# From the fifth expert round on, token rows are turned by VectorE after a trip through DRAM instead of by TensorE

## The chip, the core and the metric

One Trainium2 chip, one core of it. The engines are TensorE (PE; its weight loads are listed apart as PEld), VectorE (DVE), ScalarE (ACT), GpSimd (POOL) and SyncE (SP), which issues most DMAs. Each engine works through its own instructions in program order. The metric is the device time of one execution in microseconds (us).

## What is computed

Attention over 8 sequences of 576 tokens with 8 heads gives 4608 rows of 512 numbers. Each row goes to exactly one of 8 experts, by taking the highest gate logits of all (token, expert) pairs first until an expert has its 576 tokens:

```python
x = attn_out.transpose(0, 2, 1, 3).reshape(B * S, H * D)      # 4608 x 512
logits = x @ w_gate
order = np.argsort(-logits.flatten())
for idx in order:
    tok, e = idx // E, idx % E
    if assigned[tok] >= 0 or counts[e] >= cap: continue       # cap = 576
    assigned[tok] = e; counts[e] += 1
for e in range(E):
    mask = assigned == e
    out[mask] = np.maximum(x[mask] @ w1[e], 0.0) @ w2[e]      # 512 -> 1024 -> 512
```

## The kernel before

**Attention** fills about the first 200 us. It leaves the rows in DRAM (`xd`) and the gate logits in SBUF. **The expert stage** follows, in eight rounds `r` = 0 to 7, each of one expert: which expert fills up next, and with which tokens, is known only from the rounds before it.

A round has two products on TensorE. GEMM1 (`first`, L1387) makes `ph` from the turned rows `xh`, `xl` and the weights `w1h`, `w1l`: 8 blocks `f` of hidden units by two halves `j` of the tokens (256 and 320), 12 matmuls each. GEMM2 (L1432, L1435, L1437) makes `py` from `hb` and `w2h`, `w2l`: five tiles `m` of tokens (four of 128, one of 64) by 8 blocks `f`, 112 matmuls. Values are split into a high part (rounded by ScalarE) and a low part (the difference, by VectorE), so each product has three matmuls: ScalarE makes `w1h`, `w2h`, `xh`, the high half of `hb`; VectorE makes `w1l`, `w2l`, `xl`, the low half of `hb`.

Beside the products of a round run four chains of small work:

- **The search** for a later expert (`search`, `step`): two passes of four steps. In each, TensorE counts by 9 matmuls (`pz<-G,ohr`, L820) how many tokens lie above 16 thresholds, and VectorE (`step`, L857 to L870) turns the counts (`Q`), picks a threshold (`delta`), and makes the flags `G` for the next count. `above_base` then adds the threshold to `base` and lays out the next ones (`kb`) on VectorE. `copies` makes `ohr`, four copies of a mask.
- **The list** of an expert's tokens (`settle`, `listing`): VectorE works out flags `ge`, TensorE ranks them (`pz<-ge`, L1078, L1079), VectorE makes `oa` and six `ob`, TensorE places them (`ptx<-rx,ob`), VectorE reads `idx`.
- **The rows** (`gather`): GpSimd gathers five tiles of rows `xg` from `xd` by `idx` (L1336), TensorE turns each by four transposes into PSUM (`ptx<-const,xg`, L1350), ScalarE takes `xh` and VectorE `xl` from there. A round's rows are gathered and turned during GEMM2 of the round before it.
- **The weights**: SP loads them in 256 KB pieces `raw` (L1230).

The order of all this is set while the kernel is built: `Schedule` takes every operation with its cost, its dependences and a boost, runs them through a model of the engines, and writes each engine's instructions in the order found. On the chip the order is then fixed.

## Time and profile before

| | before |
|---|---|
| three runs | 672.52, 675.93, 676.17 us; median 675.93 us |
| the profiled execution's own time | 669.58 us |
| its span | 667.4 us |
| TensorE, VectorE, ScalarE, GpSimd busy in it | 94 %, 70 %, 43 %, 31 % |
| GEMM1 of rounds 3 and 4 | 386.1 to 413.7 us, 443.6 to 471.2 us |
| GEMM2 of rounds 3 and 4 | 413.7 to 443.6 us, 471.2 to 501.1 us |
| GEMM2 of rounds 5, 6 and 7 | 528.7 to 556.7 us, 583.1 to 611.1 us, 636.7 to 662.3 us |

The table's windows begin and end where TensorE passes from one product to the other. Busy time of TensorE is modelled at the ends of matmuls, so how long something takes there is best read from the start of one instruction to the start of the next.

### The profile page before, as it was taken

The page shows a single profiled execution, that of the slowest core. Times are in us where ns is not written, and L with a number is a line of the kernel's source. Part 1 is how long each engine was busy: PE and PEld are TensorE (multiplying, and loading weights), DVE is VectorE, ACT ScalarE, POOL GpSimd, SP SyncE. Part 2 cuts the span into 40 slices and gives each one's busy share as a digit, 9 for nine tenths or more (in the row PEclk, how much of TensorE's full clock was granted, in tenths as well). Part 3 has the DMA queues.
Part 4 walks back from the last instruction along what each step waited for, and adds up shares of the span by engine and source line. Part 5 has one row for each costly group of instructions (what it writes and reads, how often), then busy time and mean ns, then how long its engine had stood idle before and what let it go on. Part 6 is the DMA issues. An engine that isn't in the chain of part 4 may idle for free.

```text
span 667.4 us, 19062 instructions
## 1 busy us (share of the span) xinstructions
PE 630.1 (94%) x7517; PEld 550.4 (82%) x7519; DVE 468.6 (70%) x1582; ACT 287.5 (43%) x638; POOL 209.5 (31%) x316
## 2 busy tenths in 40 slices
PE   7898799999749999999999999999999999999996
PEld 6777788878636988998898799789879989988985
DVE  6668678888678784789899589779968935724210
ACT  4655465555304824754444236235423525424311
POOL 5447456664004317424104103210410321311011
PEclk9999999999857999999999999999999999999999
DMA  8988988884206937978146026214511764203001
GB/s 241 243 238 232 236 248 257 245 238 132 74 7 205 209 89 192 252 161 279 49 117 215 33 72 211 98 56 154 170 49 56 249 198 154 70 35 104 1 25 47
DMA packets 51673, 99.09 MB, mean 148 GB/s; under 512 B 7168, under 2 KB 17152, under 8 KB 51584
## 3 DMA queue, kind: packets, MB, share of 16 engines
q1 hardware_dynamic: 42240, 72.71, 37.0%
q0 software_dynamic: 9344, 25.17, 13.9%
q8 instruction: 59, 0.97, 0.6%
q14 instruction: 30, 0.25, 0.1%
HBM read 72.69 MB, written 18.87 MB: 137 GB/s over the span
## 4 chain that ended last, share of the span: by engine, by line
PE 70%; issue 13%; DVE 9%; DMA 5%; POOL 1%; ACT 1%; SPq 1%; POOLq 0%; DVEq 0%; ACTq 0%
PE ph L1387 27%; PE py L1432 20%; PE px L528 4%; PE pS L516 3%; PE px L587 2%; PE pz L820 2%; PE ptx L1350 2%; PE py L1435 2%; PE py L1437 2%; DVE xs L538 1%; POOL out L1458 1%; DMA xd<-xs 1%; PE pz L899 1%; DVE mx L451 1%; DVE L L621 1%
## 5 line engine op out<-in xcount | busy, mean ns | idle before, releaser
L1432 PE MATMUL py<-w2h,hb 128*128 128x512 f32 x512 | 170.9, 399 | 0.0
L1387 PE MATMUL ph<-xh,w1h 128*128 128x256 f32 (+1 forms) x512 | 139.6, 303 | 0.0
L1387 PE MATMUL ph<-xh,w1l 128*128 128x256 f32 (+1 forms) x512 | 136.3, 297 | 0.0
L1387 PE MATMUL ph<-xl,w1h 128*128 128x256 f32 (+1 forms) x512 | 136.0, 296 | 0.0
L1432 PEld LDWEIGHTS py<-w2h,hb 128*128 128x128 f32 x512 | 96.2, 188 | 19.2
L1212 ACT ACTIVATE hb<-ph 128x256 fp32r<-128x256 f32 (+2 forms) x192 | 59.7, 346 | 99.9 <-PE ph L1387 99.0
L1432 PE MATMUL py<-w2l,hb 128*128 128x512 f32 x256 | 100.0, 391 | 0.0
L1458 POOL DMA_INDIRECT out<-y,idx x40 | 41.5, 1037 | 186.1 <-ACT y L1212 132.7
L1387 PEld LDWEIGHTS ph<-xh,w1l 128*128 128x128 f32 x512 | 91.8, 190 | 0.0
L1387 PEld LDWEIGHTS ph<-xh,w1h 128*128 128x128 f32 x512 | 91.6, 190 | 0.3
L1387 PEld LDWEIGHTS ph<-xl,w1h 128*128 128x128 f32 x512 | 91.7, 190 | 0.0
L1408 DVE SCALAR_TENSOR_TENSOR hb<-ph,hb 128x320 fp32r<-128x320 f32 (+1 forms) x128 | 57.0, 452 | 27.7 <-ACT hb L1212 27.1
L470 ACT ACTIVATE E<-pS 128x384 f32<-128x384 f32 x96 | 46.1, 491 | 54.1 <-PE pS L516 52.4
L1212 ACT ACTIVATE y<-py 128x512 f32<-128x512 f32 (+1 forms) x40 | 23.9, 597 | 101.0 <-PE py L1432 84.8
L1432 PEld LDWEIGHTS py<-w2l,hb 128*128 128x128 f32 x256 | 48.3, 189 | 8.5
L516 PE MATMUL pS<-q,k 128*64 128x64 f32 x1152 | 54.0, 233 | 0.7 <-issue 0.7
L1336 POOL DMA_INDIRECT xg<-xd,idx x40 | 42.7, 1067 | 34.9 <-issue 27.3
L528 PE MATMUL px<-v,E 128*64 128x65 f32 x1152 | 49.0, 228 | 2.5 <-issue 1.8
L1213 DVE TENSOR_TENSOR xl<-ptx,xh 128x512 fp32r<-128x512 f32 (+1 forms) x36 | 22.9, 635 | 38.8 <-ACT xh L1212 38.8
L303 POOL COPY v<-v 32x520 f32<-32x520 f32 (+2 forms) x56 | 33.3, 619 | 52.1 <-DMA v<-in_vp 16.3
L528 PEld LDWEIGHTS px<-v,E 128*64 128x64 f32 x1152 | 43.5, 141 | 6.6 <-issue 4.0
L516 PEld LDWEIGHTS pS<-q,k 128*64 128x64 f32 x1152 | 46.0, 144 | 0.8 <-issue 0.8
(209 smaller groups left out, 1124.1 us busy)
## 6 DMA issues: line engine op xcount, KB each, us to landing
raw<-in_moe_w SPq DMA_DIRECT2D x128, 256.0 KB, 4.2
qs<-in_qp SPq DMA_DIRECT2D x16, 288.0 KB, 4.7
k<-in_kp SPq DMA_DIRECT2D x16, 288.0 KB, 3.4
...
w2l<-raw POOLq DMA_DIRECT2D x16, 256.0 KB, 4.8
...
```

The costliest lines, as they stand in the source:

```text
L303: f(t[:32, c0 + 1:c1 + 1], t[96:, c0:c1])
L470: e = self.op("ACT", 475, lambda j=j, pS=pS: nc.scalar.activation(self.E[:, 3 * j:3 * j + 3].rearrange("p c x -> p (c x)"), pS.tile[:, :38 ...
L516: x = nc.tensor.matmul(pS[64 * h:64 * h + 64, k, :, h], self.K[:, 32 * g:32 * g + 64], self.Q[:, g], start=False, stop=True, skip_group_ch ...
L528: x = nc.tensor.matmul(px[64 * h:64 * h + 64, c - c0, a], self.E[:, k, 64 * a:64 * a + 64], self.V[:, k, 2 * self.ui + a], start=True, sto ...
L587: x = nc.tensor.transpose(pt.tile[:, 128 * (c - c0):128 * (c - c0) + 128], xs[:, c, 2 * ui:2 * ui + 2].rearrange("p a d -> p (a d)"), C["i ...
L1212: act = lambda o, i, f=AF.Copy: nc.scalar.activation(o, i, f)
L1213: sub = lambda e, o, a, b: e.tensor_tensor(o, a, b, op=OP.subtract)
L1336: nc.gpsimd.indirect_dma_start(out=xg[:n], out_offset=None, in_=xd, in_offset=bass.IndirectOffsetOnAxis(ap=box[0][:n, m:m + 1], axis=0))
L1387: nc.tensor.matmul(o, a[:, d * 128:d * 128 + 128], b[:, d, c0:c1], start=((d, i) == pairs[0]), stop=((d, i) == pairs[-1]))
L1408: hl = op("DVE", 335 if j == 0 else 400, lambda: nc.vector.scalar_tensor_tensor(hb[:, CAP + c0:CAP + c1], o, 0.0, hb[:, c0:c1], op0=OP.max ...
L1432: nc.tensor.matmul(py, x, w, start=(f + i == 0), stop=(f == NF - 1 and i == 2))
L1458: s = nc.gpsimd.indirect_dma_start(out=out, out_offset=bass.IndirectOffsetOnAxis(ap=box[0][:n, m:m + 1], axis=0), in_=y[:n], in_offset=None)
```

## The change

For rounds `r` of at least `QUARTERS` = 4, `gather` hands each tile to the new function `spread`. The rows are gathered into one of two tiles (used in turn by the five), SP stores them in a DRAM scratch `rows`, SP loads them back by four DMAs into 32 partitions each in pieces of 512 bytes, so that one VectorE instruction, which transposes blocks of 32 x 32 (`STREAM_TRANSPOSE`), leaves the wanted layout in place. `xh` and `xl` are then made from SBUF. The features end up in another order over partitions, so `W1` of these rounds is read from a second array `in_moe_w1q`, of equal size and with equal loads.

`above_base` is issued after `step`, and from the search for round `KB` = 4 on it goes to ScalarE; the cost of a step on VectorE in the planner falls with it. `copies` goes to ScalarE in all rounds but the first. The loads of `W1` of round 1 get a latency in the planner. `POOLED` is an empty range, so its branch is never taken.

```diff
-    def above_base(self, it, last, delta):
-        if it > 0:
+    def above_base(self, it, last, scalar):
+        nc, pw, delta = self.tc.nc, self.pw, self.delta
+        if it == 0:
+            self.base = delta
+        else:
             nb = pw.tile([128, 1], F32, name="base")
-            nc.vector.tensor_tensor(nb, self.base, delta, op=OP.add)
+            if scalar:
+                nc.scalar.activation(nb, delta, AF.Identity, bias=self.base)
+            else:
+                nc.vector.tensor_tensor(nb, self.base, delta, op=OP.add)
             self.base = nb
         if it < 2:
             kt = self.kstep(it + 2, last)
-            nc.vector.tensor_scalar(self.kb, kt, self.base, None, op0=OP.add)
+            if scalar:
+                nc.scalar.activation(self.kb, kt, AF.Identity, bias=self.base)
+            else:
+                nc.vector.tensor_scalar(self.kb, kt, self.base, None, op0=OP.add)
...
-                g = [chain("DVE", T_S + (725 if it == 3 and not v else -805 if it == 3 else 0), dve, [p], early)]
+                cost = T_S + (725 if it == 3 and not v else -805 if it == 3 else 0) - (250, 400, 150, 0)[it] * (r >= KB)
+                g = [chain("DVE", cost, dve, [p, *g[1:]], early)]
+                if it < 3 and r >= KB:
+                    g.append(chain("ACT", (190, 370, 190)[it], lambda v=v, it=it: R.above_base(it, v, True), g, early))
...
-                src = w1[bass.ds(E[r], 1), f].rearrange("o p d f -> p (o d f)")
+                src = (w1 if r < QUARTERS else w1q)[bass.ds(E[r], 1), f].rearrange("o p d f -> p (o d f)")
...
-        ld = op("SP", 60, load, [*deps, *old], dma=T_W)
+        ld = op("SP", 60, load, [*deps, *old], dma=T_W, lat=T_L if n == "1" and r == 1 and r in gate else 0)
...
-            oc = chain("DVE", 440, lambda: R.copies(R.oh), [lv])
+            oc = (chain("ACT", 1055, lambda: R.copies(R.oh, nc.scalar), [lv]) if r else
+                  chain("DVE", 640, lambda: R.copies(R.oh, nc.vector), [lv]))
...
+    def spread(r, m, n, a, b, wx, full, ix, box):
+        rows, k = XG[NM + m % 2], n // 32
+        xg = XG[m][:, :128 * k]
+        def get():
+            nc.gpsimd.indirect_dma_start(out=rows[:n], out_offset=None, in_=xd,
+                                         in_offset=bass.IndirectOffsetOnAxis(ap=box[0][:n, m:m + 1], axis=0))
+        g = op("POOL", 1250, get, [ix, *XU[NM + m % 2]], B_G, lat=T_B)
+        back = ROWS[r % 2][m]
+        sd = op("SP", 400, lambda: nc.sync.dma_start(back[:n], rows[:n]), [g, *RU.get((r - 2, m), [])], B_R, dma=T_W)
+        def move():
+            for q in range(4):
+                nc.sync.dma_start(xg[32 * q:32 * q + 32].rearrange("t (x c) -> t x c", x=k),
+                                  back[:n, 128 * q:128 * q + 128].rearrange("(x t) c -> t x c", t=32))
+        ld = op("SP", 1600, move, [sd, *XU[m]], B_R, dma=T_W)
+        RU[r, m] = [ld]
+        XU[NM + m % 2] = [sd]
+        t = op("DVE", 130 + 7 * n, lambda: nc.vector.transpose(xg, xg), [ld], B_T)
...
+        s0 = op("ACT", full, lambda: act(a, xt), [t, *wx], B_T)
+        s1 = op("DVE", full + 100, lambda: sub(nc.vector, b, xt, a), [s0], B_T)
```

What the planner made of it stands in the order of the instructions. On **VectorE**, in GEMM2 of round 3, the rows of round 4 and the search for round 5 meet. The first five rows of before are the last of `w1l` and of the rows, `Q` begins the first search step of this GEMM2, and `G` ends it:

```order
L1213 TENSOR_TENSOR w1l_4042<-raw_4014,w1h_4026 128x512 [waits DMAHW5_49]
L1213 TENSOR_TENSOR w1l_4043<-raw_4015,w1h_4027 128x512 [waits DMAHW6_49]
L1213 TENSOR_TENSOR xl<-ptx_4007,xh 128x4x128 [waits Activation_49] x2
L1213 TENSOR_TENSOR xl<-ptx_4007,xh 128x4x64 [waits Activation_49]
L857 STREAM_TRANSPOSE Q<-pz 128x128 [waits PE_49]
L859 TENSOR_REDUCE q<-Q 128x8 [waits DVE_49]
L862 TENSOR_SCALAR junk,flag<-q 128x8 [waits DVE_49]
L864 STREAM_TRANSPOSE F<-flag 128x32 [waits DVE_49]
L867 TENSOR_SCALAR F_7551,delta<-F 128x32 [waits DVE_49]
L834 SCALAR_TENSOR_TENSOR G<-V,delta,const_65 128x36x16 [waits DVE_49]
```

The same place of the change:

```order
L1224 TENSOR_TENSOR xl<-xg_4063,xh 128x4x128 [waits Activation_49]
L1462 SCALAR_TENSOR_TENSOR hb_4075<-ph_4014,hb_4075 128x320 [waits Activation_49]
L1411 STREAM_TRANSPOSE xg_4064<-xg_4064 128x512 [waits DMAHW2_49,DMAHW1_49,DMAHW3_49,DMAHW0_49,DMASW3_49]
L1411 STREAM_TRANSPOSE xg_4065<-xg_4065 128x512 [waits DMAHW6_49,DMAHW5_49,DMAHW7_49,DMAHW4_49,DMASW4_49]
L866 STREAM_TRANSPOSE Q<-pz 128x128 [waits PE_49]
L868 TENSOR_REDUCE q<-Q 128x8 [waits DVE_49]
L871 TENSOR_SCALAR junk,flag<-q 128x8 [waits DVE_49]
L873 STREAM_TRANSPOSE F<-flag 128x32 [waits DVE_49]
L876 TENSOR_SCALAR F_7502,delta<-F 128x32 [waits DVE_49]
L835 SCALAR_TENSOR_TENSOR G<-V,delta,const_65 128x36x16 [waits DVE_49]
L1224 TENSOR_TENSOR xl<-xg_4064,xh 128x4x128 [waits Activation_49]
```

The transposes of the third and fourth tile (`xg_4064`, `xg_4065`) now stand directly ahead of the first `Q`, with waits for the DMAs that bring these tiles; those of the first and second stand among the last `hb` of GEMM1, and that of the fifth after the second `G`. The seven last `w1l`, which stood ahead of `Q`, now lie between the search steps.

On **TensorE**, at the start of GEMM1 of round 4, `pz<-ge` ranks the tokens of round 5. Before it stood in the fifth block of GEMM1 (`w1h_4025`):

```order
L1387 MATMUL ph_4002<-xh,w1l_4041 128x256
L1387 MATMUL ph_4002<-xl,w1h_4025 128x256
L1078 LDWEIGHTS const_64
L1078 MATMUL pz<-ge,const_64 128x72
L1079 LDWEIGHTS const_64
L1079 MATMUL pz<-ge,const_64 128x72
L1387 MATMUL ph_4002<-xh,w1h_4025 128x256
```

The same two matmuls in the change, with the end of GEMM2 of round 3 ahead of them:

```order
L1491 MATMUL py_4016<-w2l_4061,hb_4075 64x512
L1489 MATMUL py_4016<-w2h_4045,hb_4075 128x512
L1441 MATMUL ph_4011<-xh,w1h_4030 128x256 x4
L1441 MATMUL ph_4011<-xh,w1l_4046 128x256 x4
L1441 MATMUL ph_4011<-xl,w1h_4030 128x256 x4
L1441 MATMUL ph_4012<-xh,w1h_4031 128x256 x4
L1441 MATMUL ph_4012<-xh,w1l_4047 128x256 x4
L1087 LDWEIGHTS const_64
L1087 MATMUL pz<-ge,const_64 128x72
L1088 LDWEIGHTS const_64
L1088 MATMUL pz<-ge,const_64 128x72
```

They moved ahead by three blocks. Of the eight counts of a search, which lay half in a GEMM2 and half in the GEMM1 after it, all eight now lie in the GEMM2, one after every 9 to 15 matmuls `py`, in the searches for rounds 4, 5 and 6. The transposes `ptx<-const,xg` are gone from GEMM2 of rounds 3 to 6.

On **GpSimd** the gathers of round 4 stood in one piece:

```order
L1336 DMA xg_4052<-xd,idx 128x512 [waits DMASW3_49,DVE_49,PE_49]
L1336 DMA xg_4053<-xd,idx 128x512 [waits DMASW4_49,PE_49]
L1336 DMA xg_4054<-xd,idx 128x512 [waits DMASW5_49,PE_49]
L1336 DMA xg_4055<-xd,idx 128x512 [waits DMASW6_49,PE_49]
L1336 DMA xg_4056<-xd,idx 64x512 [waits DMASW7_49,PE_49]
```

In the change they are these, of which `DMAHW` names a wait for a DMA that SP issued:

```order
L1395 DMA xg_4067<-xd,idx 128x512 [waits DMASW3_49,DMASW5_49,DVE_49,PE_49]
L1395 DMA xg_4068<-xd,idx 128x512 [waits DMASW4_49]
L1395 DMA xg_4067<-xd,idx 128x512 [waits DMAHW0_49,DMASW3_49]
L1395 DMA xg_4068<-xd,idx 128x512 [waits DMAHW1_49,DMASW6_49,DMASW4_49]
L1395 DMA xg_4067<-xd,idx 64x512 [waits DMAHW4_49,DMASW7_49,DMASW5_49]
```

The third to fifth now wait for the stores of the first to third, since there are only two row tiles.

## Rows read from the trace of the kernel before

**Rows 1.** The page: busy time of each engine; TensorE's granted clock in 40 slices.

```profile
PE 630.1 (94%) x7517; PEld 550.4 (82%) x7519; DVE 468.6 (70%) x1582; ACT 287.5 (43%) x638; POOL 209.5 (31%) x316
...
PEclk9999999999857999999999999999999999999999
```

**Rows 2.** Busy time by stage: window, length, PE, PEld, DVE, ACT, POOL, PEclk, DMA.

```profile
443.60:471.20 27.60, 27.60 (x245) 27.19 (x241) 25.42 (x96) 13.26 (x34) 3.27 (x4) 1.00 0.42 125
471.20:501.10 29.90, 29.90 (x180) 23.32 (x178) 22.38 (x68) 8.89 (x19) 8.68 (x13) 1.00 0.30 107
...
528.70:556.70 28.00, 28.00 (x134) 22.41 (x133) 12.36 (x29) 8.50 (x17) 9.15 (x13) 1.00 0.58 190
...
636.70:662.30 25.60, 25.60 (x114) 20.44 (x112) 1.17 (x2) 2.94 (x6) 4.16 (x8) 1.00 0.11 36
```

**Rows 3.** Timeline of PE at a transpose in GEMM2 (start, length, instruction).

```profile
475.08 0.39 PE L1432 MATMUL py<-w2h,hb 128*128 128x512 f32 x1
475.31 0.60 PE L1350 MATMUL ptx<-const,xg 128*128 128x128 f32 x4
...
475.98 0.40 PE L1432 MATMUL py<-w2l,hb 128*128 128x512 f32 x1
```

**Rows 4.** VectorE, 440:560, groups by shape: busy us, mean ns.

```profile
L1132 DVE TENSOR_TENSOR ob<-si,const 128x384 bf16<-128x384 int16 x12 | 4.7, 448 | 0.0
...
L857 DVE STREAM_TRANSPOSE Q<-pz 128x128 f32<-128x128 f32 x13 | 4.0, 312 | 4.7 <-PE pz L820 4.7
...
L864 DVE STREAM_TRANSPOSE F<-flag 128x32 f32<-128x32 f32 x13 | 2.7, 211 | 0.5
...
L951 DVE COPY ohr<-oh 128x1152 bf16<-128x1152 bf16 x1 | 0.7, 745 | 0.0
...
L845 DVE TENSOR_TENSOR base<-base,delta 128x1 f32<-128x1 f32 x3 | 0.5, 152 | 0.0
```

**Rows 5.** Timeline of VectorE in round 4: list, then two search steps.

```profile
462.00 0.29 DVE L1086 TENSOR_TENSOR_SCAN scan<-const,pz 128x72 f32<-128x72 f32 x1
...
468.26 0.33 DVE L1177 SCALAR_TENSOR_TENSOR idx<-t 64x5 int32<-64x5 f32 x2
...
484.94 0.69 DVE L1213 TENSOR_TENSOR xl<-ptx,xh 128x512 fp32r<-128x512 f32 x1 [1.84 <-ACT xh L1212]
...
487.84 0.32 DVE L857 STREAM_TRANSPOSE Q<-pz 128x128 f32<-128x128 f32 x1 [0.34 <-PE pz L820]
...
489.12 0.82 DVE L834 SCALAR_TENSOR_TENSOR G<-V,delta,const 128x576 bf16<-128x576 f32 x1
...
489.86 0.23 DVE L850 TENSOR_SCALAR kb<-const,delta 128x16 f32<-128x16 f32 x1
...
490.97 0.32 DVE L857 STREAM_TRANSPOSE Q<-pz 128x128 f32<-128x128 f32 x1 [0.88 <-PE pz L820]
```

**Rows 6.** Timeline of GpSimd: the gathers of one round.

```profile
469.37 1.00 POOL L1336 DMA_INDIRECT xg<-xd,idx  x1 [4.18 <-issue]
470.67 1.43 POOL L1336 DMA_INDIRECT xg<-xd,idx  x1 [0.30 <-issue]
```

**Rows 7.** DMA issues, 440:447, 468:477, 525:540: KB, median us to landing.

```profile
raw<-in_moe_w SPq DMA_DIRECT2D x1, 256.0 KB, 2.7
...
raw<-in_moe_w SPq DMA_DIRECT2D x5, 256.0 KB, 4.0
xg<-xd,idx POOLq DMA_INDIRECT x5, 4.6
...
xg<-xd,idx POOLq DMA_INDIRECT x5, 5.3
out<-y,idx POOLq DMA_INDIRECT x1, 6.6
```

**Rows 8.** An idle PE and the clock after it, in the attention stage.

```profile
79.76 0.22 PE L504 MATMUL pm<-k,q 128*64 128x64 bf16 x2 [1.88 <-issue]
...
80.00:84.00 4.00, 4.00 (x105) 3.92 (x101) 2.30 (x7) 1.45 (x3) 3.85 (x7) 0.60 0.68 209
```

More of the change, by code (lines that the diff above doesn't have):

```diff
@@ L42 @@
 RAW1, D_R, NQ, AHEAD_W = 8, 262, (2, 2), (3, 4)
-ADDED, T_A, T_G = (("2", 0), ("1", 1), ("2", 1)), 4500, 4500
+KB, QUARTERS, POOLED, T_B, B_R = 4, 4, range(0), 2500, 20000
+ADDED, T_A, T_G, T_L = (("2", 0), ("1", 1), ("2", 1)), 4500, 4500, 3500
 NS, B_E, DIRECT = (2, 2), 3000, 7
-B_C = (0, 2500, 20000, 20000, 20000, 20000, 20000, 20000)
+B_C = (0, 2500, *(20000,) * 6)
 P_U, B_A, B_K, B_V, B_P, TOL_A, TOL_B, TOL_C, TOL_D = 4680, 15400, -5200, 14500, -105500, 650, 650, 300, 800
@@ L872, in step @@
         self.flags(V, delta, self.kstep(1, last) if it == 0 else self.kb)
-        if it == 0:
-            self.base = delta
-        self.above_base(it, last, delta)
     def search_alone(self, V, oh, last):
@@ L946, in bits, with copies @@
             nc.vector.tensor_reduce(self.who[:, c0:c1], b, axis=AX.X, op=OP.add)
-    def copies(self, oh):
+    def copies(self, oh, eng):
         self.ohr = self.pw.tile([128, NCH // 4, 4, 4 * NE], BF, name="ohr")
         src = oh.rearrange("p (j c) e -> p j (c e)", c=4)[:, :, None, :].to_broadcast([128, NCH // 4, 4, 4 * NE])
-        self.tc.nc.vector.tensor_copy(self.ohr, src)
+        if eng is self.tc.nc.scalar:
+            eng.activation(self.ohr, src, AF.Copy)
+        else:
+            eng.tensor_copy(self.ohr, src)
     def alone(self):
@@ L1179, in indices, with moe @@
         return idx
-def moe(tc, ctx, C, R, xd, w1, w2, out):
+def moe(tc, ctx, C, R, xd, ROWS, w1, w1q, w2, out):
     nc = tc.nc
@@ L1202, in moe @@
     WH, WL = ({n: ring(pw, [128, 512], F32R, "w" + n + x, NF) for n in ("1", "2")} for x in "hl")
-    XG = ring(pw, [128, DM], F32, "xg", NM)
+    XG = [pw.tile([128, DM // (1 + (i == 4))], F32, name=f"xg{i}") for i in range(NM + 2)]
+    XU = [[] for _ in XG]
     XH, XL = (pw.tile([128, ND, CAP], F32R, name=n) for n in ("xh", "xl"))
@@ L1206, in moe @@
     Y = ring(pw, [128, DM], F32, "y", 3)
+    RU = {}
     R.pa, fill = PYR.tiles[1], PHR[0].tiles[1]
@@ L1242, in weights @@
             use.append(lo)
+        elif n == "2" and r >= 2 and f in POOLED:
+            lo = op("POOL", 1350, lambda: sub(nc.gpsimd, l, raw, h), [ld, hi, *oldl], B_W)
+            use += [hi, lo]
         else:
@@ L1262, in search @@
                 early = 20000 if r == 1 and 4 * v + it < 1 else None
-                p = chain("PE", T_P, R.counts, g, early)
+                p = chain("PE", T_P, R.counts, g if it == 0 else g[:1], early)
                 def dve(v=v, it=it):
                     R.step(it, v)
+                    if it < 3 and r < KB:
+                        R.above_base(it, v, False)
                     if it == 3 and v == 0:
@@ L1332, in gather @@
         for m, n in enumerate(MSZ):
-            xg, old, use = XG.take()
+            a, b = (x[:, :, 128 * m:128 * m + n] for x in (XH, XL))
+            wx = x_users.get((r - 1, 0 if m < 2 else 1), [])
+            full = 500 if n == 128 else 290
+            if r >= QUARTERS:
+                done.append(spread(r, m, n, a, b, wx, full, ix, box))
+                continue
+            slot = m if m < 4 else NM
+            xg, old, XU[slot] = XG[slot], XU[slot], []
+            use = XU[slot]
             def get(xg=xg, n=n, m=m):
@@ L1345, in gather, with turn @@
             pt = pt.rearrange("p (d x) -> p d x", d=ND)
-            a, b = (x[:, :, 128 * m:128 * m + n] for x in (XH, XL))
-            def turn(pt=pt, xg=xg, n=n):
+            xv = xg.rearrange("n (d p) -> n d p", d=ND)
+            def turn(pt=pt, xv=xv, n=n):
                 for d in range(ND):
-                    nc.tensor.transpose(pt[:, d, :n], xg[:n, 128 * d:128 * d + 128], C["identf"][:n, :n])
+                    nc.tensor.transpose(pt[:, d, :n], xv[:n, d], C["identf"][:n, :n])
             t = op("PE", 440 if n == 128 else 380, turn, [g, *old], B_T)
@@ L1355, in gather @@
                 turns.append(t)
-            full = 500 if n == 128 else 290
-            wx = x_users.get((r - 1, 0 if m < 2 else 1), [])
             s0 = op("ACT", full, lambda pt=pt, a=a, n=n: act(a, pt[:, :, :n]), [t, *wx], B_T)
@@ L1362, in gather @@
         return done
+    def spread(r, m, n, a, b, wx, full, ix, box):
[15 more added lines that the diff above has]
+        t = op("DVE", 130 + 7 * n, lambda: nc.vector.transpose(xg, xg), [ld], B_T)
+        xt, a, b = (*(y.rearrange("p d (x i) -> p d x i", i=32) for y in (b, a)), xg.rearrange("p (x d i) -> p d x i", d=ND, i=32))[::-1]
+        s0 = op("ACT", full, lambda: act(a, xt), [t, *wx], B_T)
+        s1 = op("DVE", full + 100, lambda: sub(nc.vector, b, xt, a), [s0], B_T)
+        XU[m] = [s0, s1]
+        return s0, s1
     last, turns, gemm0, puts = [None], [], {}, {}
@@ L1513, in layout @@
         "in_moe_w1": w1.reshape(NE, DM // 128, 128, FF // 128, 128).transpose(0, 3, 2, 1, 4),
+        "in_moe_w1q": w1.reshape(NE, 4, DM // 128, 32, FF // 128, 128).transpose(0, 4, 1, 3, 2, 5).reshape(NE, FF // 128, 128, DM // 128, 128),
         "in_moe_w2": w2,
@@ L1548, in build @@
         xd = dp.tile([N, DM], F32, name="xd")
+        rows = [[dp.tile([128, DM], F32, name=f"rows{i}_{m}") for m in range(NM)] for i in range(2)]
         Lt = cp.tile([128, NCH, NE], F32, name="Lt")
@@ L1553, in build @@
         with ExitStack() as c2:
-            moe(tc, c2, C, R, xd, T["in_moe_w1"], T["in_moe_w2"], out)
+            moe(tc, c2, C, R, xd, rows, T["in_moe_w1"], T["in_moe_w1q"], T["in_moe_w2"], out)
 def kernel(**inputs):
```

1 line of the change is left out of this document (removed).

## Prediction

> **What bounds the kernel now.** I read the page first: TensorE is busy 94 % of the span, at full clock but for one dip in the attention stage and one near the start of the expert stage [rows 1]. Then I cut the expert stage where TensorE passes from GEMM1 to GEMM2 [rows 2]. In each of these windows TensorE is busy for the whole of it and its clock is 1.00, so up to 662 us an instruction taken from TensorE comes off the time, and an instruction that TensorE has to wait for is added to it. VectorE comes second: 25.42 of 27.6 us in GEMM1 of round 4 and 22.38 of 29.9 us in GEMM2 [rows 2], together 47.8 of 57.5 us, or 83 %. From round 5 on, where no search is left, it has room (12.36 of 28.0 us). So there are two questions: how much TensorE time the turns cost, and whether what takes their place makes TensorE wait in rounds 2 to 6.
>
> **Removed: the turns on TensorE.** GEMM2 of round 5 has the same 112 matmuls as that of round 7, and five turns more; it lasts 28.0 us against 25.6 us [rows 2]. So five turns cost 2.4 us. The timeline agrees: from the matmul ahead of a turn to the second one behind it are 475.98 - 475.08 = 0.90 us [rows 3], of which two matmuls would take 2 x 25.6 / 112 = 0.46 us; that leaves 0.44 us for one turn, 2.2 us for five. Turns of four rounds go (those of rounds 4 to 7, in GEMM2 of rounds 3 to 6): 4 x 2.4 = **9.6 us** off, between 8.8 and 10.3.
>
> **Added on VectorE: five transposes a round.** The trace has no transpose of 512 columns. One of 128 columns takes 312 ns, one of 32 takes 211 ns [rows 4]: 101 ns for 96 columns, so 512 columns come to 312 + 384 x 1.05 = 0.72 us, the 256 columns of the last tile to 0.45 us; a round gets 4 x 0.72 + 0.45 = 3.3 us. The upper bound is four of the 128-column instructions, 1.25 us a tile. I take 0.72 us, since startup is paid once. Off VectorE come `ohr` (745 ns) and, in a search, four `kb` (0.23 us [rows 5]) and four `base` (0.15 us [rows 4]), 1.5 us. So VectorE stands at 47.8 + 3.3 - 2.2 = 48.9 us of a round that is 55.1 us long, 89 %: it fits, but little is left where the work comes in a lump.
>
> **Moved: the list of tokens, to the start of GEMM1.** The placing matmuls want six `ob` soon after the ranks. The cost in `listing` is 110 + 26 x 6 = 266 ns for one; the trace has 448 ns [rows 4]. Six are up to 1.1 us later than planned, less where one begins as the last ends, and TensorE stands at the placing in its order. I take 0.4 us (0 to 1.1), in GEMM1 of rounds 3, 4, 5 and 6: **1.6 us**.
>
> **Moved: all eight counts of a search into one GEMM2.** The search is a closed circle: a count, a step on VectorE (2.1 us from `Q` to the end of `G`, 487.84 to 489.94 [rows 5]), the next count. Counts stand about 3.1 us apart there, and VectorE waited 0.88 us before the second `Q` [rows 5]. That gap takes one `w1l` or the fifth tile's transpose, not more; a delay ahead of the first step is therefore paid once and not won back. In GEMM2 of round 2 the turns stay and three steps come in: 22.4 us of VectorE's work as in the row of round 4, and 6.3 us, in about 31 us. I take **1.0 us** of waiting (0.3 to 2).
>
> **Added: three transfers in series, ahead of the first step.** In GEMM2 of rounds 3 and 4 VectorE cannot begin the first `Q` before the transposes of the third and fourth tile, and these wait for DMAs. The times from the start of GEMM1 are as follows. From `scan` to the end of `idx` are 6.6 us (462.00 to 468.59 [rows 5]); the ranks ahead of it are now about 2.5 us after the start, so `idx` ends at 9.1. The first gather starts 0.8 us after `idx` and the second 1.3 us after that [rows 6]. For the fourth tile follow: gather of the second tile, its store (the tile buffer must be free), its own gather, store and load. A gather takes 4.6 us here, a 256 KB load by SP 2.7 us alone and 4.0 us among others [rows 7]; stores and pieced loads are not in this trace, and I bound them by these two. The fourth tile is there at 9.1 + 2.1 + 2 x 4.6 + 3 x 2.7 = 28.5 at the earliest, and at 32.4 with 4.0 us; I take 30.5. GEMM1 without its counts ends at about 26.5, the first count at 29.6. With the tile at 30.5, the transpose ends and `Q` begins at 31.2, the flags are there at 33.4 and the second count was due at 29.6 + 2.75 = 32.3: TensorE waits 1.1 us (0 at the early end, 3.0 at the late one). With hand-overs I take 1.2 us, in two rounds **2.4 us**. In rounds 5 and 6 no search follows, and the tiles are wanted only 20 us later. The first two tiles (at 9.1 + 0.8 + 4.6 + 2 x 4.0 = 22.5 and 1.3 us later) stand ahead of the last `hb`, which GEMM2 wants some 4 us after its start, near 31: no cost.
>
> **Costed at nothing.** `W1` from the second array: the same 256 KB loads. The 25 SP transfers a round share a queue with the weights, whose loads behind them are wanted a GEMM later. `kb` and `base` on ScalarE: wanted one count later, about 1 us after the count ends; ScalarE is busy 8.89 of 29.9 us there [rows 2], and if all eight came late by a `kb` of 0.23 us, a search would cost 1.8 us. `ohr` on ScalarE: made some 15 us before the first count. Some low parts of round 1's `W1` change places; if one is late, up to the 0.69 us of such a subtraction (`xl` [rows 5]).
>
> **The sum.** -9.6 + 1.6 + 1.0 + 2.4 = **-4.6 us**. The profiled execution took 669.58 us and would take 665.0 us. It lay 6.35 us below the median of the runs, 675.93 us; against the median the forecast is **671.3 us**, -0.7 %. Its own range, with stalls from 2.5 to 8 us, is 668.8 to 674.3.
>
> **Rival: all of the gain stays.** The planner left room, the transfers come in at 2.7 us, TensorE never waits: 675.93 - 9.6 = 666.3 us. For it speaks the DMA share of 0.30 to 0.42 in these windows [rows 2]; against it the lump of transposes right ahead of the first `Q`.
>
> **Rival: VectorE sets the pace.** A transpose of 512 columns takes four times the 128-column one, 1.25 us [rows 4]. Two of them stand ahead of the first `Q` (2 x 0.53 us) and the fifth in a step whose gap is used up (0.3 us): 1.4 us in each of two rounds, 671.3 + 2.8 = 674.1 us, no change that can be told. For it speaks that VectorE reaches 89 % even at my price; against it, that startup would be paid four times in one instruction.
>
> On this the Trainium skill, page "VectorE: DVE Perf Modes", speaks against the change: its section "Rules for kernel authors" sends 128 x 128 transposes to TensorE where PSUM will do as destination, since (section "The three transpose paths") VectorE turns only 32 x 32 blocks. That section gives 311 ns for 128 x 128 on VectorE, and an estimate from it is 4 x 0.311 = 1.24 us a tile, the price of this rival; the 312 ns of `Q` [rows 4] agree. Its 390 ns on TensorE would make a turn 1.56 us, where the trace has 0.44 us [rows 3]; the measurement decides.
>
> **Rival: slower, by late transfers.** Five transfers in series bring the fourth tile. If each takes 1 us more than I took, the tile is 5 us later, TensorE waits 5 us more in two rounds, and the time is 671.3 + 10 = 681 us. It is slower by 0.5 % from 0.8 us each. For it speaks that gathers took 5.3 us and a scatter 6.6 us between 525 and 540 us [rows 7], and that SP issues stores and loads in order among weight loads that wait for buffers. Against it: the DMA shares named. It would be made worse by the clock: an idle TensorE of 1.88 us was followed by a stretch of 4 us at 0.60 [rows 8], between its two levels of 1.2 and 2.4 GHz, 1.6 us lost each time.
>
> **How the numbers follow.** The forecast has 0.48, all of the gain 0.20, VectorE's pace 0.15, late transfers 0.17. A measurement of this kernel can tell about 0.5 %, 3.4 us: faster means under 672.5 us, slower over 679.3 us. Three quarters of the forecast, all of the first rival and a tenth of the second are faster: 0.36 + 0.20 + 0.02 = 0.58. Of the third rival 0.15 are slower, with 0.02 for mishaps of the second: 0.17. The rest, 0.25, is the same. The range takes in the full gain with 2.3 us for the scatter of the runs (664.0), and ends where late transfers begin to be slower (679.5).
>
> **What would show it.** GEMM2 of rounds 5 and 6 should last 25.6 to 26 us instead of 28.0. `STREAM_TRANSPOSE` of `xg` should take 0.7 us; 1.25 us would be the second rival. In GEMM2 of rounds 3 and 4 TensorE should idle about 1 us ahead of the second count and nowhere for 2 us; idling before several counts means VectorE's pace, one gap of 4 us and more, with the transpose of `xg` released by a DMA, means late transfers. About 0.4 us should be lost at the placing in each GEMM1. A clock below 1.00 in these windows, or a store of 256 KB over 5 us, would make the forecast wrong.

## The result: slower, and the profile after

| | before | changed |
|---|---|---|
| median of the runs beside each other | 674.22 us (668.2 to 676.17, 4 runs) | 681.51 us (678.33 to 684.92, 4 runs) |
| ratio to before | | 1.011, 95 % interval 1.0064 to 1.0157 |
| span of the profiled execution | 667.4 us | 683.1 us |

The change makes the kernel slower by 1.1 %. Now and then an execution is slow; the ratios, here and below, leave such runs out and are not the quotients of the medians. The forecast was 671.3 us and faster; the measured time lies outside the range of 664.0 to 679.5, on the side of the third rival.

The profiled execution of the changed kernel is the slowest of its four. Its attention stage, which the change does not touch, reached the expert stage some 5 us later than before, so the stages are compared by their lengths. (The differences below add up to +9.2 us in this one pair of executions; the ratio of the runs gives 7.4 us.) These are the windows of GEMM2 of round 2, GEMM1 and GEMM2 of rounds 3, 4 and 5, and GEMM2 of round 6 (window, its length, then busy time of PE, PEld, DVE, ACT, POOL, and the clock, DMA share and GB/s):

```profile
362.70:395.60 32.90, 31.54 (x206) 24.38 (x205) 28.81 (x100) 12.49 (x27) 8.00 (x12) 1.00 0.32 100
395.60:422.10 26.50, 26.47 (x213) 26.28 (x212) 20.67 (x61) 15.34 (x37) 6.30 (x7) 1.00 0.70 221
422.10:457.50 35.40, 30.60 (x187) 23.58 (x186) 27.52 (x96) 10.07 (x23) 5.63 (x9) 0.95 0.27 89
457.50:483.80 26.30, 26.30 (x214) 26.21 (x212) 20.99 (x64) 15.11 (x37) 6.44 (x7) 1.00 0.72 227
483.80:521.00 37.20, 31.70 (x187) 24.26 (x186) 27.52 (x96) 10.07 (x23) 5.60 (x9) 0.91 0.24 82
521.00:547.30 26.30, 26.30 (x213) 26.20 (x212) 19.09 (x56) 14.06 (x36) 5.72 (x7) 1.00 0.75 237
547.30:574.00 26.70, 26.01 (x116) 20.56 (x115) 14.00 (x35) 7.42 (x15) 5.68 (x9) 1.00 0.60 182
...
601.30:626.80 25.50, 25.50 (x114) 20.65 (x113) 8.49 (x17) 7.02 (x14) 4.45 (x8) 1.00 0.19 59
```

| | before | after | difference |
|---|---|---|---|
| GEMM2 of round 2 | 29.9 | 32.9 | +3.0 |
| GEMM1 of round 3 | 27.6 | 26.5 | -1.1 |
| GEMM2 of round 3 | 29.9 | 35.4 | +5.5 |
| GEMM1 of round 4 | 27.6 | 26.3 | -1.3 |
| GEMM2 of round 4 | 29.9 | 37.2 | +7.3 |
| GEMM1 of round 5 | 27.6 | 26.3 | -1.3 |
| GEMM2 of round 5 | 28.0 | 26.7 | -1.3 |
| GEMM1 of round 6 | 26.4 | 27.3 | +0.9 |
| GEMM2 of round 6 | 28.0 | 25.5 | -2.5 |

Of the rows of before, [rows 2] has GEMM1 and GEMM2 of round 4 and GEMM2 of rounds 5 and 7; the rest of the first column is from the same view. Where no search runs the turns were saved as reckoned: GEMM2 of round 6 has the length of bare matmuls. The 1.1 to 1.3 us that three GEMM1 lost are the counts that moved into GEMM2: by the trace of before it was three of the eight that lay in GEMM1 (in round 3 at 389.06, 392.96 and 396.54; the fifth began at 385.81, at the very end of GEMM2), and GEMM1 of round 6, which had no count, took 26.4 us. The loss is in GEMM2 of rounds 3 and 4, where TensorE, busy throughout before, is busy for 30.6 of 35.4 and 31.7 of 37.2 us, at a mean clock of 0.95 and 0.91. What TensorE waited for from 300 us on in the changed kernel is a short list; these are its three longest entries (us in total, times, the longest):

```profile
PE pz L821 <- DVE G L835: 11.4, 3, 5.5
PE ph L1441 <- DVE hb L1462: 0.7, 1, 0.7
PE py L1486 <- ACT y L1223: 0.7, 1, 0.7
```

All three waits of `pz` are for the flags `G` of a search step. One, of 1.2 us, is in GEMM2 of round 2; the two others are 4.8 and 5.5 us long. The first of the long ones, on the timeline of TensorE (start, length, instruction, idle time before it and what ended it):

```profile
427.80 0.39 PE L1486 MATMUL py<-w2h,hb 128*128 128x512 f32 x1
432.96 0.60 PE L821 MATMUL pz<-G,ohr 128*128 128x64 bf16 x9 [4.77 <-DVE G L835]
```

The other side of it is VectorE in the same stretch:

```profile
418.33 0.71 DVE L1411 STREAM_TRANSPOSE xg<-xg 128x512 f32<-128x512 f32 x1 [1.23 <-DMA xg<-rows]
...
422.90 0.71 DVE L1411 STREAM_TRANSPOSE xg<-xg 128x512 f32<-128x512 f32 x1 [3.55 <-DMA xg<-rows]
...
428.94 0.71 DVE L1411 STREAM_TRANSPOSE xg<-xg 128x512 f32<-128x512 f32 x1 [2.42 <-DMA xg<-rows]
430.22 0.71 DVE L1411 STREAM_TRANSPOSE xg<-xg 128x512 f32<-128x512 f32 x1 [0.56 <-DMA xg<-rows]
430.86 0.27 DVE L866 STREAM_TRANSPOSE Q<-pz 128x128 f32<-128x128 f32 x1
...
432.08 0.82 DVE L835 SCALAR_TENSOR_TENSOR G<-V,delta,const 128x576 bf16<-128x576 f32 x1
```

The transposes of `xg` at 418.33, 422.90, 428.94 and 430.22 are the four large tiles of round 4, and each was held by a DMA. The first count of the search was done long before (it began at 424.90); its `Q` starts at 430.86, the moment the fourth tile is turned, and the flags of this step release TensorE at 432.96. Behind such a gap the clock falls. These are the window right after the first gap and the two after the second (columns as above, the clock third from the end):

```profile
433.00:437.00 4.00, 4.00 (x19) 3.25 (x19) 3.75 (x12) 1.03 (x3) 1.33 (x2) 0.57 0.23 79
495.00:499.00 4.00, 3.70 (x17) 3.02 (x17) 3.75 (x13) 0.91 (x4) 1.31 (x2) 0.50 0.23 83
499.00:503.00 4.00, 4.00 (x22) 2.94 (x21) 1.55 (x8) 0.33 (x1) 0.00 (x0) 0.71 0.00 0
```

A clock of 0.50 is the lower of the two levels of 1.2 and 2.4 GHz; 0.57 and 0.71 are means of windows that lie partly at each. In the same place before, the clock was 1.00 [rows 2]. An estimate from these windows is 4 x 0.43 = 1.7 us lost behind the first gap and 4 x 0.50 + 4 x 0.29 = 3.2 us behind the second.

### The profile page after: what moved, and what is told of

It is laid out like the page before. It is cut to its first block, busy times and chain, and to the rows that moved or that the text cites. A ratio compares the mean times of both kernels' runs of the same rounds, so it can differ in the third digit from the quotient of the medians.

```text
span 683.1 us, 19125 instructions
## 1 busy us (share of the span) xinstructions
PE 624.8 (91%) x7437; PEld 544.7 (80%) x7439; DVE 473.8 (69%) x1573; ACT 300.0 (44%) x667; POOL 210.4 (31%) x316
## 5 line engine op out<-in xcount | busy, mean ns | idle before, releaser
L1441 PE MATMUL ph<-xh,w1h 128*128 128x256 f32 (+1 forms) x512 | 138.2, 300 | 0.7 <-DVE hb L1462 0.7
L1486 PEld LDWEIGHTS py<-w2h,hb 128*128 128x128 f32 x512 | 98.0, 191 | 20.9 <-ACT y L1223 1.1
L1224 DVE TENSOR_TENSOR w2l<-raw,w2h 128x512 fp32r<-128x512 f32 x48 | 31.7, 686 | 24.2 <-ACT w2h L1223 22.9
L1395 POOL DMA_INDIRECT xg<-xd,idx x20 | 21.7, 1087 | 67.8 <-DMA rows<-xg 52.9
```

The lines of the kernel that those rows point to most:

```text
L1224: sub = lambda e, o, a, b: e.tensor_tensor(o, a, b, op=OP.subtract)
L1395: nc.gpsimd.indirect_dma_start(out=rows[:n], out_offset=None, in_=xd, in_offset=bass.IndirectOffsetOnAxis(ap=box[0][:n, m:m + 1], axis=0))
L1441: nc.tensor.matmul(o, a[:, d * 128:d * 128 + 128], b[:, d, c0:c1], start=((d, i) == pairs[0]), stop=((d, i) == pairs[-1]))
L1486: nc.tensor.matmul(py, x, w, start=(f + i == 0), stop=(f == NF - 1 and i == 2))
```

## Experiments

All kernels start from the changed one. The times are medians of 4 to 10 runs; the before beside each group lay between 670.5 and 674.6 us, so the ratios are what to compare.

| run | time (us) | ratio to before | 95 % interval |
|---|---|---|---|
| the change | 681.51 | 1.011 | 1.0064 to 1.0157 |
| turns back on TensorE | 674.86 | 1.0022 | 0.9982 to 1.0063 |
| trip alone | 679.92 | 1.0103 | 1.0066 to 1.014 |
| own tiles | 680.43 | 1.0111 | 1.0054 to 1.0167 |
| no trip | 664.64 | 0.9824 | 0.9751 to 0.9898 |
| stores first | 673.51 | 1.0018 | 0.9988 to 1.0048 |
| own tiles, long durations | 667.55 | 0.994 | 0.9909 to 0.997 |
| shared tiles, long durations | 675.55 | 1.005 | 1.0024 to 1.0075 |
| last two rounds | 671.24 | 1.0002 | 0.9975 to 1.0028 |
| no trip, turned twice | 663.07 | 0.9895 | 0.9826 to 0.9963 |
| own tiles, short durations | 680.08 | 1.0123 | 1.0045 to 1.0201 |
| own tiles, three rounds | 668.54 | 0.9978 | 0.9937 to 1.0018 |
| own tiles, longer durations | 662.48 | 0.9904 | 0.9869 to 0.994 |

What lies ahead of the first GEMM1, nearly all of it the attention stage that no edit touches, took 206 to 217 us in the profiled executions and blurs the times. The stretch from the start of GEMM2 of round 2 to the end of GEMM2 of round 6 is free of it, in one execution each: 254.9 us before, 264.1 in the change, 259.8 with turns back, 246.8 with no trip, 249.0 with no trip and turned twice, 247.6 with own tiles and longer durations.

The theory from the trace was the third rival, late transfers: tiles that come after their place in VectorE's fixed order hold the first search step, and with it TensorE. Its rivals were VectorE's load, and the thresholds and copies that went to ScalarE.

### Which part of the change: turns back, and the trip alone

```diff
-KB, QUARTERS, POOLED, T_B, B_R = 4, 4, range(0), 2500, 20000
+KB, QUARTERS, POOLED, T_B, B_R = 4, 8, range(0), 2500, 20000
```

> All rounds turn their rows on TensorE again; thresholds from round 4 on and the mask copies stay on ScalarE. Late transfers (the third rival of the prediction): without the trip through DRAM no transpose stands ahead of a search step, so the gaps of 4.9 and 5.6 us in GEMM2 of rounds 3 and 4 go and the time is near that of before, 672 to 677 us. ScalarE (thresholds or copies late): the gaps and the loss of 7 us stay, 680 to 683 us.

Measured: 674.86 us, the same as before within the interval. By the times the loss is in the trip. The two long gaps are gone; what TensorE waits for in GEMM2 now are weights:

```profile
PE py L1486 <- DVE w2l L1224: 1.6, 3, 1.1
PE py L1486 <- ACT w2h L1223: 0.9, 1, 0.9
```

The profiled execution shows that what is left of the change is not free: GEMM2 of rounds 3, 4 and 5 are 31.2, 31.5 and 29.2 us long, 1.2 to 1.6 us longer than before. In each of them ScalarE waits 1.8 to 2.1 us for the load of a `w2` piece, and TensorE then waits for a part of `w2` made late; in round 3:

```profile
412.94 0.63 ACT L1223 ACTIVATE w2h<-raw 128x512 fp32r<-128x512 f32 x1 [1.76 <-DMA raw<-in_moe_w]
```

The copies on ScalarE are not what holds TensorE here. `ohr`, 745 ns on VectorE [rows 4], takes longer on ScalarE, by this group of the changed kernel (busy, mean ns), but in this run it begins at 419.06 and 478.40, behind the last waits for weights of these GEMM2 (up to 416.67 and 476.01):

```profile
L958 ACT ACTIVATE ohr<-oh 128x1152 bf16<-128x1152 bf16 x2 | 2.3, 1159 | 0.0
```

Why these loads come later in this order was not followed.

The other half, with `copies` on VectorE and thresholds there in all rounds:

```diff
-KB, QUARTERS, POOLED, T_B, B_R = 4, 4, range(0), 2500, 20000
+KB, QUARTERS, POOLED, T_B, B_R = 8, 4, range(0), 2500, 20000
-            oc = (chain("ACT", 1055, lambda: R.copies(R.oh, nc.scalar), [lv]) if r else
-                  chain("DVE", 640, lambda: R.copies(R.oh, nc.vector), [lv]))
+            oc = chain("DVE", 440, lambda: R.copies(R.oh, nc.vector), [lv])
```

The latency `T_L` was also set to 0.

> The trip through DRAM from round 4 on as in the change, but thresholds and mask copies on VectorE as before. Late transfers: one long gap ahead of the second count remains in GEMM2 of rounds 3 and 4 where the transposes stand ahead of the step, and the time is 678 to 686 us. ScalarE: the gaps go, 664 to 670 us. VectorE's load: 2 us more per round on VectorE, so slower than the change, 684 us or more, with waits at several counts.

Measured: 679.92 us, as slow as the change. The time was as expected, the place was not: the planner laid another order, in which the long gaps do not exist and the loss is spread over GEMM1 of rounds 4 and 5 (32.2 and 30.5 us), with waits such as this:

```profile
PE ph L1441 <- DVE w1l L1224: 1.6, 1, 1.6
```

So the trip costs this much in two different orders, and with the thresholds on either engine. The run does not tell late transfers from VectorE's load.

### Late transfers or VectorE: the order held, the trip left out

Four tiles are gathered into their own tiles and turned there, with no store and no load, which leaves their features mixed up; only the fifth makes the trip. The planner still sees the trip, so the order of PE, VectorE, ScalarE and GpSimd is that of the change.

```diff
-        rows, k = XG[NM + m % 2], n // 32
+        rows, k = XG[m if m < 4 else NM], n // 32
-        sd = op("SP", 400, lambda: nc.sync.dma_start(back[:n], rows[:n]), ...)
+        sd = op("SP", 400, lambda: nc.sync.dma_start(back[:n], rows[:n]) if m == 4 else None, ...)
-            for q in range(4):
+            for q in range(4 if m == 4 else 0):
```

> The order held as in the change; the four tiles of 128 rows are gathered into their own tiles and turned in place with no store and no load, so their features are mixed up (the output is not the reference's); only the fifth tile makes the trip. Late transfers: the first gap goes entirely, TensorE waits only for what VectorE's pace and the list cost, 664 to 669 us, and no more than 3 us below the run with own tiles. VectorE's load: unchanged work on VectorE, 679 to 683 us.

Measured: 664.64 us, 1.8 % faster than before. VectorE has the same work in the same order, and nearly all waits of TensorE are gone:

```profile
PE pz L821 <- DVE G L835: 0.6, 2, 0.4
```

This settles it between the two: with the data there in time, the order of the change is good and the gain comes (8.1 us in the stretch, where 9.6 were forecast). The run also takes the trip's own traffic away; that lateness and not traffic is what counts is shown further down, where all transfers are made and only their order or the order of the work differs. To see how much room VectorE has, the same kernel got every transpose of the rows twice:

```diff
-        t = op("DVE", 130 + 7 * n, lambda: nc.vector.transpose(xg, xg), [ld], B_T)
+        t = op("DVE", 130 + 7 * n, lambda: (nc.vector.transpose(xg, xg), nc.vector.transpose(xg, xg)), [ld], B_T)
```

> As the run without the trip (order held, four tiles turned where they were gathered, the output is not the reference's), but every transpose by VectorE is issued twice, 3.2 us more on VectorE in each of four rounds. If VectorE has the room that 89 % leaves, the time rises by no more than 0 to 4 us over the 664.6 of that run, with waits of 0.6 to 1.5 us at the second count. If VectorE sets the pace, by 7 us or more.

Measured: a ratio of 0.9895 against 0.9824, 4.8 us more, just over the expected 0 to 4, with intervals that overlap; the waits for flags grew by 1.1 us:

```profile
PE pz L821 <- DVE G L835: 1.7, 4, 0.6
```

So 3.3 us more on VectorE in each of four rounds cost TensorE about 1 us of waits for flags and a few us in all (2.2 in the stretch). The second rival, VectorE's pace, falls.

### Why the tiles are late: five transfers in series

In the changed kernel these are the gathers of the four large tiles of round 4 on GpSimd (start, length, instruction, idle time before and its end):

```profile
405.64 0.99 POOL L1395 DMA_INDIRECT xg<-xd,idx  x1 [0.75 <-issue]
406.94 1.03 POOL L1395 DMA_INDIRECT xg<-xd,idx  x1 [0.30 <-issue]
414.75 1.24 POOL L1395 DMA_INDIRECT xg<-xd,idx  x1 [6.78 <-DMA rows<-xg]
416.30 1.23 POOL L1395 DMA_INDIRECT xg<-xd,idx  x1 [0.30 <-issue]
```

and SP's queue beside them (start of the first, time to the end of the last, x their number):

```profile
410.10 2.95 SPq L1401 DMA_DIRECT2D rows<-xg  x2
414.15 3.66 SPq L1405 DMA_DIRECT2D xg<-rows  x8
...
419.15 0.37 SPq L1401 DMA_DIRECT2D rows<-xg  x1
...
422.53 0.33 SPq L1401 DMA_DIRECT2D rows<-xg  x1
424.66 3.85 SPq L1405 DMA_DIRECT2D xg<-rows  x8
```

GEMM1 of round 3 began at 395.6. The third gather goes out at 414.75, once the first store has landed (issued at 410.10; its load could follow at 414.15, 4.0 us later); the fourth at 416.30. The store of the fourth tile is issued at 422.53, 6.2 us after its gather began, and its load follows about 4 us later, as the second half of the eight at 424.66.

The first try was to take the two waits for stores out: each large tile is gathered into its own tile, with the order held.

```diff
-        rows, k = XG[NM + m % 2], n // 32
+        rows, k = XG[m if m < 4 else NM], n // 32
```

> The order of every engine held as in the change; only, each tile of 128 rows is gathered into its own tile, so that the third and fourth gather wait for no store. Late transfers: two of the five transfers in series go, about 9 us; the fourth tile comes at about 26 us after the start of GEMM1 instead of 34.6, before the first count; the gaps of 4.9 and 5.6 us and the clock dips behind them (1.3 and 2.1 us) go, 666 to 671 us. VectorE's load or ScalarE: no change, 679 to 683 us.

Measured: 680.43 us, no gain; this expectation failed, though late transfers were the cause. The gathers do go out at once:

```profile
399.02 0.96 POOL L1395 DMA_INDIRECT xg<-xd,idx  x1 [0.31 <-issue]
```

but SP's queue shows why that did not help:

```profile
400.13 3.80 SPq L1401 DMA_DIRECT2D rows<-xg  x2
405.66 3.66 SPq L1405 DMA_DIRECT2D xg<-rows  x8
409.57 0.98 SPq L1241 DMA_DIRECT2D raw<-in_moe_w  x2
410.66 0.37 SPq L1401 DMA_DIRECT2D rows<-xg  x1
...
414.12 4.59 SPq L1405 DMA_DIRECT2D xg<-rows  x8
```

GEMM1 of round 3 begins at 386.4 here. The third tile was gathered from 399.02 on, and its store is issued at 410.66: it stands in SP's order behind the loads of the first two tiles, which begin only when the first store has landed, and behind two weight loads. The fourth store stands behind two more. The transposes come no earlier, counted from GEMM1 (420.43 - 386.4 = 34.0 us for the fourth tile, 430.22 - 395.6 = 34.6 in the change):

```profile
418.31 0.71 DVE L1411 STREAM_TRANSPOSE xg<-xg 128x512 f32<-128x512 f32 x1 [3.70 <-DMA xg<-rows]
...
420.43 0.71 DVE L1411 STREAM_TRANSPOSE xg<-xg 128x512 f32<-128x512 f32 x1 [1.41 <-DMA xg<-rows]
421.06 0.27 DVE L866 STREAM_TRANSPOSE Q<-pz 128x128 f32<-128x128 f32 x1
```

Two chains of almost the same length led to the late tile, the shared row tiles and SP's order; taking out one left the other. (SP's order was not changed alone, with the shared tiles.) The next run kept the own tiles and moved two instructions on SP alone, the stores of the third and fourth tile, which are issued where the gather is issued:

```diff
             nc.gpsimd.indirect_dma_start(out=rows[:n], ...)
+            if m in (2, 3):
+                nc.sync.dma_start(back[:n], rows[:n])
```

> As the run with own tiles (order of PE, VectorE, ScalarE and GpSimd held), but SP gets the stores of the third and fourth tile ahead of the load of the second tile, and so ahead of the four weight loads that wait for their buffers; the loads of these tiles stay behind them. If SP's queue is what kept the own tiles from helping, the two loads begin as soon as the weight loads are issued, 2 to 3 us earlier; the gaps ahead of the second count shrink from 4.4 and 5.5 us to 1.5 to 3 us, 673 to 677 us. If the transfers themselves are slow wherever they stand, no change, 679 to 682 us.

Measured: 673.51 us, the time that was expected of SP's queue. Its rows there:

```profile
407.65 0.85 SPq L1398 DMA_DIRECT2D rows<-xg  x2
...
410.74 2.15 SPq L1241 DMA_DIRECT2D raw<-in_moe_w  x4
413.00 4.95 SPq L1407 DMA_DIRECT2D xg<-rows  x8
```

The two stores (407.65) now stand between the loads of the first and second tile, and the loads of the third and fourth begin at 413.00, right after the weights, 26.3 us after the start of GEMM1 (386.7) instead of 27.7. With the same transfers and the same work, these two instructions a round, moved on SP, brought the ratio from 1.0111 to 1.0018, about 6 us. The gaps themselves shrank less than expected, from 4.23 and 5.39 us to 3.05 and 3.44, where 1.5 to 3 were expected: the tiles are still late. The rest of the gain lies in the clock, which stayed at 1.00 behind the first of these gaps, and in a wait of 1.5 us for `y` in GEMM2 of round 5 that is gone.

### Why the planner put them there: its durations

The planner reckons a gather at 1.25 + 2.5 us, and a store or a load at about 2.7 us (1.1 + 0.73 + 0.9). In the trace of the changed kernel a gather took 4.4 to 6.2 us to its store, and a store about 4 us. The next runs gave it other durations, and let it lay all orders anew:

```diff
-KB, QUARTERS, POOLED, T_B, B_R = 4, 4, range(0), 2500, 20000
+KB, QUARTERS, POOLED, T_B, B_R = 4, 4, range(0), 4000, 20000
-        sd = op("SP", 400, ..., B_R, dma=T_W)
+        sd = op("SP", 400, ..., B_R, dma=T_W, lat=1200)
-        ld = op("SP", 1600, move, [sd, *XU[m]], B_R, dma=T_W)
+        ld = op("SP", 1600, move, [sd, *XU[m]], B_R, dma=T_W, lat=700)
```

With the two shared tiles:

> The two shared row tiles of the change, only the planner reckons with longer transfers (gather +1.5 us, store +1.2 us, load +0.7 us) and lays the orders anew. Lateness against the plan: the single long gaps go, but the tiles come so late that the search is broken up; 667 to 675 us, faster than the change by 6 us or more. If the five transfers in series cannot be hidden by any order, 677 to 683 us.

Measured: 675.55 us, by the ratios 4 us less than the change, where 6 or more were expected, and still 0.5 % slower than before: no single long gap, but six waits at counts (9.5 us), with the search drawn apart over GEMM2 of round 2 (38.5 us) and GEMM1 of rounds 3 and 4. In this order, at least, the five transfers in series are not hidden.

With the same durations and own tiles that the planner knows of (`own = m if m < 4 else NM` for the tile, its dependences, and `XU`):

> Own tiles, known to the planner, and a planner that reckons with longer transfers (gather +1.5 us, store +1.2 us, load +0.7 us), so it lays all engines' orders anew. If lateness against the planned order is the cause, no step of the search stands behind a late tile and the gain of 9.6 us mostly comes: 664 to 670 us. If VectorE or the DMA load is the bound, it stays over 675 us.

Measured: 667.55 us, 0.6 % faster than before. With own tiles known to the planner, but the short durations of the change:

> Own tiles known to the planner, which lays the orders anew, but still with the short durations of the change. If the durations matter, the tiles come after their place in the order again and it stays slower than the run with own tiles and long durations (667.6 us), 670 to 678 us. If only the shared tiles mattered, 664 to 669 us.

Measured: 680.08 us, as slow as the change and over the expected range, with two waits of 5.5 and 5.2 us at counts again. So neither the tiles nor the durations alone bring the gain; the order must be laid for transfers that take as long as they take. With durations longer still (`T_B` 4500, store 2500, load 1500):

> Own tiles, and durations longer still in the planner (gather +2.0 us, store +2.5 us, load +1.5 us over the change). The gaps of 1.8 and 2.0 us ahead of the second count that remained with the long durations go: 662 to 666 us. If the order is now so late that the search is broken up, 667 to 672 us.

Measured: 662.48 us, a ratio of 0.9904 (0.9869 to 0.994). This version beats both kernels. On VectorE, in GEMM2 of round 3 (from 411.5 on), the search steps no longer wait for late tiles:

```profile
419.37 0.71 DVE L1413 STREAM_TRANSPOSE xg<-xg 128x512 f32<-128x512 f32 x1 [2.15 <-DMA xg<-rows]
...
420.57 0.30 DVE L866 STREAM_TRANSPOSE Q<-pz 128x128 f32<-128x128 f32 x1
...
425.29 1.62 DVE L1413 STREAM_TRANSPOSE xg<-xg 128x512 f32<-128x512 f32 x3
```

Only the second tile holds VectorE, ahead of a first step that has time; the third to fifth are turned in one piece (425.29, x3) behind the second step, when they are long there. TensorE's longest wait from 300 us on is now 0.6 us; its waits for flags, 11.4 us in the change, are down to 0.4:

```profile
PE ptx L1160 <- POOL rx L1146: 0.6, 1, 0.6
...
PE pz L821 <- DVE G L835: 0.4, 1, 0.4
```

### Fewer rounds

The trip only for rounds 6 and 7, whose tiles no search follows (`QUARTERS` = 6):

> The trip only for the rows of rounds 6 and 7 (QUARTERS = 6), which no search follows. Late transfers have nothing to hold up there: GEMM2 of rounds 5 and 6 lose their turns, 2 x 2.4 = 4.8 us, less the 1.9 us of waits that the change showed at the end of GEMM2 of round 5 and in GEMM1 of round 6; 669 to 673 us. If something else in the trip costs time (the second W1, more DMA traffic), 674 us or more.

Measured: 671.24 us against 670.99 us, no change, where 669 to 673 was expected: the time fits, but the before beside it is 3.6 us below that of the first group, and no gain is left. The saved turns are there (GEMM2 of rounds 5 and 6 last 25.7 and 25.5 us), but other losses eat them. Two are waits:

```profile
PE ph L1441 <- DVE hb L1462: 1.5, 1, 1.5
PE pz L821 <- ACT ohr L958: 0.7, 1, 0.7
```

The first is in GEMM1 of round 6, where a late first tile stands in VectorE's order ahead of a low half of `hb`; GEMM1 is 2.0 us longer than before for it. The second is `ohr`, made on ScalarE. GEMM2 of rounds 3 and 4, where turns and the ScalarE edits meet, are 1.1 and 3.0 us longer than before; 1.3 of the 3.0 are counts that came over from GEMM1 of round 5 (26.3 instead of 27.6 us), and the rest is as in the run with turns back.

With own tiles and long durations, and round 7 left on TensorE:

```diff
-            if r >= QUARTERS:
+            if QUARTERS <= r < 7:
-                src = (w1 if r < QUARTERS else w1q)[bass.ds(E[r], 1), f].rearrange("o p d f -> p (o d f)")
+                src = (w1q if QUARTERS <= r < 7 else w1)[bass.ds(E[r], 1), f].rearrange("o p d f -> p (o d f)")
```

> Own tiles and long durations, but the trip only for rounds 4, 5 and 6; round 7 turns its rows on TensorE. In the run with four rounds GEMM1 of round 6 was 3.0 us longer than before and GEMM2 of round 6 2.5 us shorter, so giving up the last one should cost nothing: 665 to 668 us. If the wait in GEMM1 of round 6 is not from these tiles, 669 to 671 us.

Measured: 668.54 us, between the two expected ranges, ratio 0.9978 (0.9937 to 1.0018), within the intervals not to be told from four rounds (0.994). In the profiled executions GEMM1 of round 6 fell from 29.5 to 27.4 us and GEMM2 of round 6 rose from 25.5 to 28.0, as was argued. It stays open whether round 7 is worth it.

## Why the prediction was wrong, point by point

- **The turns, -9.6 us: right.** GEMM2 of round 6 went from 28.0 to 25.5 us, and without the trip the kernel is 1.8 % faster (interval 1.0 to 2.5 %, where 9.6 us are 1.4 %).
- **The transposes on VectorE: right.** 0.72 us was forecast for 512 columns by the slope of [rows 4]; the row of the changed kernel has 711 ns:

```profile
L1411 DVE STREAM_TRANSPOSE xg<-xg 128x512 f32<-128x512 f32 x16 | 11.4, 711 | 30.1 <-DMA xg<-rows 30.1
```

  VectorE's load was right too: 20.99 + 27.52 = 48.5 us in GEMM1 and GEMM2 of round 4, forecast 48.9.

  The Trainium skill, page "VectorE: DVE Perf Modes", section "The three transpose paths", has 311 ns for 128 x 128 (bf16) on VectorE, from which 1.24 us was estimated for four of them; this case's row does not agree for one instruction of 512 columns.
- **The placing, +1.6 us: too much.** GEMM1 of rounds 3 to 5 lost 1.1 to 1.3 us with the counts gone, which is what the counts took (they are now 26.3 to 26.5 us long, and GEMM1 without counts took 26.4 before); there is no room for a loss of 0.4 us in each. What brought the six `ob` in time was not followed further.
- **GEMM2 of round 2, +1.0 us: near.** One wait for flags of about 1.2 us; GEMM2 of round 2 and GEMM1 of round 3 together are 1.9 us longer.
- **The late tile, +1.2 us a round: the step that failed.** The fourth tile was forecast at 30.5 us after the start of GEMM1, 32.4 at the latest; it was turned at 34.6. `idx` and the first two gathers came as forecast (the first at 405.64 - 395.6 = 10.0 us, forecast 9.9). What was too short is the series after it. A gather was taken at 4.6 us, the median of [rows 7]: the second took 5.8 us until its store went out (406.94 to 413.05, less an issue of 0.33) and the fourth 6.2, with four tiles and weight loads in flight. A transfer by SP was taken at 3.35 us, between the bounds: the three took 11.3 us together (412.71 to 416.30 and 422.53 to 430.22), about 3.8 each. That makes 2.8 and 1.2 us, the 4 us that were missing. The bound of 32.4 used 4.6 us for the gathers at both ends, although [rows 7] had 5.3. The forecast also counted waits for stores and left SP's order out, which gives the same lateness by a second way.
- **The price of lateness: right in kind, and dearer.** The forecast had VectorE's order, the place of the gap and its release as they came; 4.1 us later tiles gave a gap of 4.8 us instead of 1.2, and in round 4 one of 5.5. To that comes the clock, which the forecast had named as making it worse, 1.6 us each time, but left out of the sum: by the windows above about 1.7 us in round 3 and 3.2 in round 4. Longer gaps (3.6 + 4.3) and the clock (4.9), less the 0.8 of the placing that did not come, make 12.0 us, about the 11.8 by which these two rounds missed the forecast.
- **The rivals.** Late transfers had 0.17 and gave 681 us for five transfers of 1 us more each; measured were 681.5 us and about 4 us more in sum. It was the right mechanism with too small a chance: by the traces of before, a series of five transfers of which two kinds were unseen should not have had a range of only 3.9 us (28.5 to 32.4). That the time itself agrees is in part luck: the rival had no clock in its sum, and more lateness than came.

- **Rounds 5 and 6, at nothing: wrong, by less.** The forecast let the tiles come late there because no search follows. But other work stands behind them: on ScalarE `xh` of the fifth tile stands ahead of `y`, and on VectorE the first tile of round 7 ahead of a low half of `hb`, and TensorE waited 0.7 us for each. GEMM2 of round 5 lasted 26.7 us, where 25.6 to 26 was the sign.

```profile
563.60 0.42 ACT L1223 ACTIVATE xh<-xg 128x256 fp32r<-128x256 f32 x1 [6.46 <-DVE xg L1411]
595.16 0.71 DVE L1411 STREAM_TRANSPOSE xg<-xg 128x512 f32<-128x512 f32 x1 [5.09 <-DMA xg<-rows]
```

The differences in the table add up to +9.2 us, 13.8 us from the forecast's -4.6. Taken as pairs of a GEMM2 and the GEMM1 behind it, rounds 3 and 4 hold 5.0 and 6.8 of these (+4.2 and +6.0 against -0.8 forecast for each), the pair of GEMM2 of round 5 and GEMM1 of round 6 1.6, the one of round 2 0.5.

What stays open: how much of the 5.8 and 6.2 us of the second and fourth gather is the other traffic and how much the queue of GpSimd; no run took one away alone.
